# Attention plus gated FFN in one decode step: result rows by (batch, quarter of D), the FFN result moved there by fp32 selection matmuls, one store

## The chip, the cores and the metric

The kernel runs on one core of a Trainium2 chip. The metric is the device time of one execution in microseconds (us); less is better. Five runs of the kernel before gave a median of 120.75 us, from 120.64 to 121.13.

## What is computed

There are 8 batch rows of one token each, D = 512. The row is normalised, then used twice: for attention over the last 1024 positions of a K/V cache (32 query heads on 8 K/V heads of width 128), and for a gated FFN (F = 1792). The result joins the two.

```python
xn = _layernorm(x, axis=-1)                       # x: (8, 1, 512), bf16
# _A_ref: q = xn @ wq; softmax(q k^T * Dh**-0.5) v over the last W = 1024 positions; then @ wo
s = _A_ref(xn, A_k_cache, A_v_cache, A_wq, A_wo)  # wo: (4096, 512)
# _B_ref: (gelu(xn @ w_gate) * (xn @ w_up)) @ w_down     w_down: (1792, 512)
g = _silu(_B_ref(xn, B_w_gate, B_w_up, B_w_down))
return x + s * g
```

## The kernel before

**Loads.** Nearly all bytes (47.5 MB) are weights and caches that are read once. SyncE's queue (SP) issues them in one written-out order: wq and the first K slots, then V and K slots of 1 MB for 16 groups, then w_gate, w_up, w_down (1.75 MB each) and wo in six pieces of 16, 8, 4, 2, 1 and 1 rows of 128x512 (`parts`, line 488). x is loaded twice: `x_sb` for the normalisation on ScalarE's queue (line 139), and `x_res`, the x that is added at the end, on SP's queue between the second and third piece of wo (line 491).

**Order of the work.** The schedule is written by hand: every engine runs its instructions in the program's order. A prologue makes the constants and xT (the normalised x, transposed, lines 202 to 226) and q (lines 361 to 400), which is copied into `q2_all` by eight small copies (line 395). A loop over 16 groups, a group being a batch row and half of the K/V heads, turns K on TensorE (line 244), copies it (250), makes scores (270), softmax (283, 291), values (304) and normalises (lines 320 to 334). Then come `ffn_up` (403), `ffn_down` (448), and the wo product (518 to 531).

**The FFN.** `ffn_up` makes z = xn @ w_gate and u = xn @ w_up on TensorE (411), in between regroups the attention output into `og`, one 32-column block for each of the 32 row blocks of wo (353), then applies gelu on ScalarE and VectorE (423 to 435) and transposes the product into `hT`, 14 blocks of 128x32 (438). `ffn_down` multiplies the 14 blocks with w_down. The 512 columns of the result are cut in halves t: half 0 goes to PSUM partitions 0 to 31 and half 1 to partitions 64 to 95, by matmuls on different column groups of the array (`tile_position=(0, 64 * t)`, line 453), so a pair can be in the array together. Silu (465 to 474) is done once for each half on 8 partitions and gives `g_sb`.

**wo and the end.** For each row block j of wo, two matmuls of 256 columns (line 523) add to `s_ps`, half 0 on partitions 0 to 63 and half 1 on 64 to 127, with a 64-column stationary `og[:, j : j + 2, :]`. Two VectorE operations on 128 partitions multiply by the gate and add x (534, 535), and two stores write the halves, 8 rows of 512 B each, on SP's and ScalarE's queue (537, 538).

Of the kernel before, what the change touches and what calls it, by code (L numbers as in the profile page):

```python
# [8 lines left out]
ACT = mybir.ActivationFunctionType  # L9
ALU = mybir.AluOpType  # L10
AX = mybir.AxisListType
BF16 = mybir.dt.bfloat16
FP32 = mybir.dt.float32
# [3 lines left out]
def kernel(  # L17
# [13 lines left out]
    nc = tc.nc  # L31

    B, Sq, D = A_x.shape
# [11 lines left out]
    P = nc.NUM_PARTITIONS  # L45
# [10 lines left out]
    FR = F // P  # L56

    consts = ctx.enter_context(tc.tile_pool(name="consts", bufs=1))
# [21 lines left out]
        return wide.tile([P, 2 * SLOT], BF16, name="wide_slot", align_bytes=512)  # L80

    x_flat = A_x.flatten_outer_dims()
    x_sb = persist.tile([B, D], BF16, name="x_sb")
    x_res = persist.tile([P, D // 2], BF16, name="x_res")
    nc.gpsimd.memset(x_res, 0.0)

# [29 lines left out]
    def load_wo(j0, j1):  # L118
# [13 lines left out]
    k_t[1] = load_kv(A_k_cache, *groups[1])  # L132


    eps_sb = consts.tile([B, 1], FP32, name="eps_sb")
    nc.vector.memset(eps_sb, 1e-5)
    rstd = persist.tile([B, 1], FP32, name="rstd")
    nc.scalar.activation(out=rstd, in_=eps_sb, func=ACT.Sqrt)
    nc.scalar.dma_start(out=x_sb, in_=x_flat)


    ident = consts.tile([P, P], BF16, name="ident")
# [56 lines left out]
    )  # L199


    stats = persist.tile([B, nc.vector.BN_STATS_DIM], FP32, name="stats")
    nc.vector.bn_stats(out=stats, in_=x_sb)
    mv = persist.tile([B, nc.vector.BN_AGGR_DIM], FP32, name="mv")
    nc.vector.bn_aggr(out=mv, in_=stats)
    nc.scalar.activation(out=rstd, in_=mv[:, 1:2], func=ACT.Sqrt, bias=eps_sb, scale=1.0)
    nc.vector.reciprocal(out=rstd, in_=rstd)
    xhat = persist.tile([32, D], BF16, name="xhat")
    nc.vector.memset(xhat, 0.0)
    nc.vector.tensor_scalar(  # L210
        out=xhat[0:B, :],
        in0=x_sb,
        scalar1=mv[:, 0:1],
        scalar2=rstd[:, 0:1],
# [15 lines left out]
    q2_all = persist.tile([P, NHALF, B, 2, 2, HN, rep], BF16, name="q2_all")  # L230
    nc.gpsimd.memset(q2_all, 0.0)
    oT_all = persist.tile([P, B, Hq], BF16, name="oT_all")
    og = persist.tile([P, NOR + 1, 32], BF16, name="og")
    nc.vector.memset(og, 0.0)

# [105 lines left out]
    def regroup():  # L341

        zt = ffn_sb.tile([P, B * Hq], BF16, name="zt")
        nc.vector.transpose(out=zt, in_=oT_all.rearrange("p b h -> p (b h)"))
        rg = ps_a.tile([P, B, 32], FP32, name="rg_ps", tag="a")
        nc.tensor.matmul(
            rg.rearrange("p b j -> p (b j)"),
            perm,
            zt,
            start=True,  # L350
            stop=True,
        )
        nc.vector.tensor_copy(
            out=og[:, 0:NOR, 0:B], in_=rg.rearrange("p b j -> p j b")
        )


# [25 lines left out]
    for i in range(NHALF):  # L383
        qT_ps = ps_t.tile([P, rep, 2, HN, 32], BF16, name="t_ps", tag="t")
        for j in range(rep):
            for e in range(2):
                nc.tensor.transpose(
                    qT_ps[:, j, e, :, :].rearrange("p n b -> p (n b)"),
                    q_sb[:, i, j, e, :, :].rearrange("p r w -> p (r w)"),
                    ident,  # L390
                )
        for e in range(2):
            for rr in range(2):
                copy = nc.scalar.copy if rr else nc.vector.tensor_copy
                copy(  # L395
                    out=q2_all[64 * rr : 64 * rr + 64, i, :, e, rr, :, :].rearrange(
                        "p b n j -> p j n b"
                    ),
                    in_=qT_ps[64 * rr : 64 * rr + 64, :, e, :, 0:B],
                )  # L400


    def ffn_up():
        z_ps = ps_big.tile([P, 512], FP32, name="big")
        u_ps = ps_big.tile([P, 512], FP32, name="big")
        for ps, ws in ((z_ps, wg_t), (u_ps, wu_t)):
            if ps is u_ps:
                regroup()
            for k in range(NDC):
                for j in range(4):  # L410
                    nc.tensor.matmul(  # L411
                        ps[32 * j : 32 * j + 32, 0:FT],
                        xT[:, k, :],
                        ws[:, k * F + j * FT : k * F + (j + 1) * FT],
                        start=(k == 0),
                        stop=(k == NDC - 1),
                        tile_position=(0, 32 * j),
                        skip_group_check=True,
                    )
        zT = z_ps[:, 0:FT]  # L420
        uT = u_ps[:, 0:FT]
        z2 = ffn_sb.tile([P, FT], FP32, name="z2")
        nc.scalar.activation(out=z2, in_=zT, func=ACT.Square)
        nc.vector.tensor_scalar(
            out=z2, in0=z2, scalar1=0.044715, scalar2=1.0, op0=ALU.mult, op1=ALU.add
        )
        u3 = ffn_sb.tile([P, FT], FP32, name="u3")
        nc.vector.tensor_tensor(out=u3, in0=z2, in1=zT, op=ALU.mult)
        nc.scalar.activation(out=z2, in_=u3, func=ACT.Tanh, scale=0.7978845608028654)
        nc.vector.tensor_scalar(  # L430
            out=z2, in0=z2, scalar1=0.5, scalar2=0.5, op0=ALU.mult, op1=ALU.add
        )
        nc.vector.tensor_tensor(out=u3, in0=z2, in1=zT, op=ALU.mult)
        h_sb = ffn_sb.tile([P, FT], BF16, name="h_sb")
        nc.vector.tensor_tensor(out=h_sb, in0=u3, in1=uT, op=ALU.mult)

        hT = ffn_sb.tile([P, FR, 32], BF16, name="hT")
        nc.vector.transpose(
            out=hT.rearrange("p j b -> p (j b)"),
            in_=h_sb.rearrange("b (p j) -> b j p", j=FR),  # L440
        )
        return hT

    x_b = persist.tile([P, D // 2], BF16, name="x_b")
    g_sb = persist.tile([P, D // 2], FP32, name="g_sb")
    nc.vector.memset(g_sb, 0.0)

    def ffn_down(hT):
        f_ps = ps_big.tile([P, 512], FP32, name="big")
        for j in range(FR):  # L450
            for t in range(2):
                c0 = j * D + t * 256
                nc.tensor.matmul(  # L453
                    f_ps[64 * t : 64 * t + 32, 0:256],
                    hT[:, j, :],
                    wd_t[:, c0 : c0 + 256],
                    start=(j == 0),
                    stop=(j == FR - 1),
                    tile_position=(0, 64 * t),
                    skip_group_check=True,  # L460
                )
        th2 = ffn_sb.tile([P, 256], FP32, name="th2")
        for t in range(2):
            a, z = 64 * t, 64 * t + B
            nc.scalar.activation(
                out=th2[a:z, :], in_=f_ps[a:z, 0:256], func=ACT.Tanh, scale=0.5
            )
            nc.vector.tensor_scalar(
                out=th2[a:z, :], in0=th2[a:z, :], scalar1=0.5, scalar2=0.5,
                op0=ALU.mult, op1=ALU.add,  # L470
            )
            nc.vector.tensor_tensor(
                out=g_sb[a:z, :], in0=th2[a:z, :], in1=f_ps[a:z, 0:256], op=ALU.mult
            )


    for g in range(NGR + 1):
# [8 lines left out]
        if g == NGR:  # L486

            parts = [(0, 16), (16, 24), (24, 28), (28, 30), (30, 31), (31, 32)]
            wo_t = [load_wo(*q) for q in parts[:2]]
            for t in range(2):  # L490
                nc.sync.dma_start(
                    out=x_res[64 * t : 64 * t + B, :], in_=x_flat[:, t * 256 : (t + 1) * 256]
                )
            wo_t += [load_wo(*q) for q in parts[2:]]
        if g < NGR:
            score(g)
# [12 lines left out]
        if g:  # L509
            gather(g - 1)  # L510

    hT = ffn_up()
    ffn_down(hT)

    nc.vector.tensor_copy(out=x_b, in_=x_res)


    s_ps = ps_big.tile([P, 512], FP32, name="big")
    for q, (j0, j1) in enumerate(parts):
        for j in range(j0, j1):  # L520
            for t in range(2):
                c0 = (j - j0) * D + t * 256
                nc.tensor.matmul(  # L523
                    s_ps[64 * t : 64 * t + 64, 0:256],
                    og[:, j : j + 2, :].rearrange("p m b -> p (m b)"),
                    wo_t[q][:, c0 : c0 + 256],
                    start=(j == 0),
                    stop=(j == NOR - 1),
                    tile_position=(0, 64 * t),
                    skip_group_check=True,  # L530
                )
    tmp = ffn_sb.tile([P, 256], BF16, name="tmp")
    out_sb = ffn_sb.tile([P, 256], BF16, name="out_sb")
    nc.vector.tensor_tensor(out=tmp, in0=s_ps[:, 0:256], in1=g_sb, op=ALU.mult)
    nc.vector.tensor_tensor(out=out_sb, in0=tmp, in1=x_b, op=ALU.add)
    out_flat = out.flatten_outer_dims()
    nc.sync.dma_start(out=out_flat[:, 0:256], in_=out_sb[0:B, :])
    nc.scalar.dma_start(out=out_flat[:, 256:512], in_=out_sb[64 : 64 + B, :])


# [28 lines left out]
```

The softmax here doesn't subtract the row's maximum and nothing guards it: scores larger than these inputs give would overflow.

## Time and profile before

| | |
|---|---|
| median of 5 runs (lowest, highest) | 120.75 us (120.64, 121.13) |
| the profiled execution | 121.13 us, of which its span 119.5 us |
| mean granted TensorE clock | 0.90 |
| HBM read | 47.46 MB, 397 GB/s over the span |
| busy: TensorE, VectorE, ScalarE | 87.8, 64.2, 40.5 us |
| share of DMA in the chain that ended last | 52% |

In the profile's lines, times are us from the start of the span. PE is TensorE's matmuls, PEld its weight loads, DVE is VectorE, ACT ScalarE, POOL GpSimd, SPq and ACTq the queues that issue DMAs. "L523" is line 523 of the kernel, "x28" a count of instructions, and the bracket at the end of a line tells how long the engine had been idle and what it waited for. A row of 40 digits cuts the span in 40 slices of 3 us: the digit is a busy share in tenths, and for PEclk the clock that TensorE was granted in tenths of the full one. In a table by stretches, each engine's busy time is followed by its count of instructions; the last three columns are the granted clock, the DMA share and GB/s.

### The profile page before, as it was taken

Reading aid. Unit: us, or ns where it says so; the run is one execution under the profiler, and the core shown is the slowest. Engines: PE = TensorE matmul, PEld = TensorE weight load, DVE = VectorE, ACT = ScalarE, POOL = GpSimd, SP = SyncE. Lnnn points to the kernel's source line nnn. Section 1 sums busy time; section 2 is a strip of 40 time slices with the busy share of each in tenths; the row PEclk is TensorE's granted clock in tenths of the full one; section 3 lists DMA queues with packets and bytes.
Section 4 is the critical chain, followed back from the end, with each engine's and each line's share of the span. In section 5 each row is a group of like instructions: output and inputs, shape, how many; then the busy total and the mean of one; then the engine's idle time right before and its main releaser. Section 6 shows DMA issues by size and latency. Waiting matters only on the chain.

```text
span 119.5 us, 2281 instructions
## 1 busy us (share of the span) xinstructions
PE 87.8 (74%) x929; PEld 63.1 (53%) x929; DVE 64.2 (54%) x149; ACT 40.5 (34%) x78; POOL 4.3 (4%) x10
## 2 busy tenths in 40 slices
PE   0014966676999999999998797977979840554990
PEld 0004723453867876786776584665847620142870
DVE  5250644735567866866695574845847426512201
ACT  4000314692433562464355342362433303002000
POOL 7600000000000000000000000000000000000000
PEclk9999999769599999999999999999999985555579
DMA  4999999999999999999999999999999999999920
GB/s 93 431 400 461 400 431 425 428 428 422 425 428 431 422 417 431 425 428 420 428 425 428 422 422 431 431 414 428 431 431 441 418 432 446 425 430 406 397 105 3
DMA packets 6281, 47.61 MB, mean 398 GB/s; under 512 B 728, under 2 KB 1024, under 8 KB 1280
## 3 DMA queue, kind: packets, MB, share of 16 engines
q1 hardware_dynamic: 6240, 47.46, 94.7%
q8 instruction: 7, 0.11, 0.3%
q10 hardware_dynamic: 32, 0.01, 0.0%
q14 instruction: 2, 0.02, 0.0%
HBM read 47.46 MB, written 0.01 MB: 397 GB/s over the span
## 4 chain that ended last, share of the span: by engine, by line
DMA 52%; PE 29%; DVE 10%; ACT 4%; issue 1%; SPq 0%; DVEq 0%
DMA wide_slot<-in_B_w_gate_dram 18%; DMA slot<-in_A_v_cache_dram 16%; PE t_ps L244 13%; DMA wide_slot<-in_A_wo_dram 10%; DMA slot<-in_A_k_cache_dram 8%; DVE kT L250 6%; PE big L523 5%; PE sc_ps L270 4%; PE o_ps L304 3%; ACT q_all L395 2%; PE big L366 2%; DVE q_all L395 2%; ACT L283 1%; PE big L411 1%; DVE q_sb L379 1%
## 5 line engine op out<-in xcount | busy, mean ns | idle before, releaser
L250 DVE COPY kT<-t_ps 128x1024 bf16<-128x1024 bf16 x48 | 31.8, 687 | 25.2 <-PE t_ps L244 23.3
L244 PE MATMUL t_ps<-ident_f,slot 128*128 128x128 f32 x256 | 38.6, 300 | 7.0 <-DMA slot<-in_A_k_cache_dram 6.8
L244 PEld LDWEIGHTS t_ps<-ident_f,slot 128*128 128x128 f32 x256 | 30.7, 152 | 17.2 <-issue 6.8
L250 ACT COPY kT<-t_ps 128x1024 bf16<-128x1024 bf16 x16 | 16.2, 1012 | 15.1 <-PE t_ps L244 14.7
L283 ACT ACTIVATE p<-sc_ps 128x512 bf16<-128x512 f32 x16 | 9.6, 597 | 29.2 <-PE sc_ps L270 29.1
L270 PE MATMUL sc_ps<-kT,q_all 128*32 128x512 bf16 x128 | 10.1, 384 | 4.2 <-ACT q_all L395 1.8
L291 DVE STREAM_TRANSPOSE pT<-p 128x512 bf16<-128x512 bf16 x16 | 11.3, 703 | 3.1 <-ACT p L283 3.1
L304 PE MATMUL o_ps<-slot,pT 128*32 128x256 bf16 x256 | 10.4, 284 | 0.0
L324 PE MATMUL a_ps<-selr,o_sb 128*128 128x16 f32 x64 | 9.7, 264 | 0.4 <-ACT o_sb L314 0.3
L324 PEld LDWEIGHTS a_ps<-selr,o_sb 128*128 128x128 f32 x64 | 8.5, 194 | 0.6 <-ACT o_sb L314 0.6
L270 PEld LDWEIGHTS <-q_all 128*32 128x32 bf16 x128 | 3.2, 94 | 8.1 <-issue 3.2
L304 PEld LDWEIGHTS <-pT 128*32 128x32 bf16 x256 | 5.6, 97 | 2.8 <-issue 2.4
L314 ACT COPY o_sb<-o_ps 128x256 f32<-128x256 f32 x16 | 6.0, 377 | 1.3 <-PE o_ps L304 1.3
L523 PEld LDWEIGHTS <-og 128*64 128x64 bf16 x64 | 4.8, 151 | 2.8 <-DMA wide_slot<-in_A_wo_dram 2.1
L260 PE MATMUL sc_ps<-far,hot 4*128 4x512 bf16 x16 | 6.2, 385 | 0.0
L411 PE MATMUL big<-wide_slot,xT 128*32 128x448 bf16 x32 | 2.9, 503 | 4.2 <-DMA wide_slot<-in_B_w_up_dram 2.7
L220 PE MATMUL t_ps<-ident,xhat 32*128 32x32 bf16 x4 | 0.3, 194 | 7.2 <-DVE xhat L210 7.2
L320 PEld LDWEIGHTS a_ps<-ss,ones_f 128*128 128x128 f32 x32 | 5.1, 200 | 0.5 <-DVE oT_all L334 0.3
L453 PE MATMUL big<-wide_slot,hT 128*32 128x256 bf16 x28 | 3.2, 416 | 2.6 <-DMA wide_slot<-in_B_w_down_dram 2.6
L320 PE MATMUL a_ps<-ss,ones_f 128*128 128x16 f32 x32 | 5.1, 234 | 0.0
L523 PE MATMUL big<-wide_slot,og 128*64 128x256 bf16 x32 | 3.6, 420 | 1.6 <-DMA wide_slot<-in_A_wo_dram 1.6
L333 DVE RECIPROCAL rs<-a_ps 128x16 f32<-128x16 f32 x16 | 4.0, 250 | 1.4 <-PE a_ps L324 1.2
(64 smaller groups left out, 51.1 us busy)
## 6 DMA issues: line engine op xcount, KB each, us to landing
slot<-in_A_k_cache_dram SPq DMA_DIRECT2D x16, 1024.0 KB, 19.6
slot<-in_A_v_cache_dram SPq DMA_DIRECT2D x16, 1024.0 KB, 19.6
wide_slot<-in_A_wq_dram SPq DMA_DIRECT2D x2, 2048.0 KB, 13.5
wide_slot<-in_A_wo_dram SPq DMA_DIRECT2D x1, 2048.0 KB
wide_slot<-in_B_w_gate_dram SPq DMA_DIRECT2D x1, 1792.0 KB, 21.4
wide_slot<-in_B_w_up_dram SPq DMA_DIRECT2D x1, 1792.0 KB, 23.2
wide_slot<-in_B_w_down_dram SPq DMA_DIRECT2D x1, 1792.0 KB, 25.0
slot<-in_A_wo_dram SPq DMA_DIRECT2D x1, 1024.0 KB
```

The costliest lines, as they stand in the source:

```text
L244: nc.tensor.transpose(kp[:, c * P : (c + 1) * P], kw[:, rp * P : (rp + 1) * P], ident_f)
L250: copy(out=kT_t[g][:, t * 8 * P : (t + 1) * 8 * P], in_=kp.bitcast(BF16))
L260: nc.tensor.matmul(sc, hot.rearrange("n r q -> n (r q)"), far, start=True, stop=False, skip_group_check=True,)
L270: nc.tensor.matmul(sc[32 * t : 32 * t + 32, :], q2_all[:, i, b, e, :, :, :].rearrange("w r n j -> w (r n j)"), kT[:, :, 32 * t : 32 * t + ...
L283: nc.scalar.activation(out=p, in_=sc_t[g], func=ACT.Exp, scale=inv_sqrt_dh, accum_out=acc)
L291: nc.vector.transpose(out=pT, in_=p)
L304: nc.tensor.matmul(o_ps[32 * u : 32 * u + 32, :], pT_t[g][:, m * 32 : (m + 1) * 32], v_t[g][:, m * 256 : (m + 1) * 256], start=(m < 4), st ...
L314: nc.scalar.copy(out=o_sb, in_=o_ps)
L320: nc.tensor.matmul(a_ps[:, 0, :], ones_f, ss_t[g], start=True, stop=True, skip_group_check=True)
L324: nc.tensor.matmul(a_ps[:, 1, :], o_t[g][:, r * Dh : (r + 1) * Dh], selr[:, r, :], start=(r == 0), stop=(r == 1), skip_group_check=True,)
L395: copy(out=q2_all[64 * rr : 64 * rr + 64, i, :, e, rr, :, :].rearrange("p b n j -> p j n b"), in_=qT_ps[64 * rr : 64 * rr + 64, :, e, :, 0:B],
L523: nc.tensor.matmul(s_ps[64 * t : 64 * t + 64, 0:256], og[:, j : j + 2, :].rearrange("p m b -> p (m b)"), wo_t[q][:, c0 : c0 + 256], start= ...
```

## The change

The result is held on 32 partitions, one for each (batch, quarter of D), row 4b + q, in place of 8 batch rows with two halves of D on two groups of partitions.

- **x.** `x_sb` has 32 rows, of which every fourth holds a batch row; VectorE fills it with zeros first, and it is loaded by two issues on ScalarE's queue. So `xhat`, and the copies that took columns 0 to 7 of a 32-column block, work with every fourth column (lines 353 and 395). `x_res` holds x in the (batch, quarter) form, loaded by two issues of 16 rows of 256 B. Its memset and the copy `x_b` go.
- **Shifted stationaries.** `og` keeps batch b in column 4b of a block. A 32-column window that begins q columns earlier puts batch b into output row 4b + q. So each row block of wo is multiplied by four matmuls of 128 columns, one for each quarter, all adding to the same 32x128 result.
- **Even rows in an own tile.** Row blocks 0, 2, ... 26 add to a second PSUM tile on partitions 32 to 63 (column group 32), all others, with 28 to 31, to a first one on partitions 0 to 31. An even and the next odd row block take turns. The even half is multiplied by the gate and gets x added (`early`) ahead of the last sum.
- **FFN result.** `ffn_down` makes 14 matmuls of 512 columns on one column group. The 32x512 result is copied to SBUF in fp32 by ScalarE, and four fp32 matmuls with a shifted identity (`push`, made by GpSimd) move its quarters to rows 4b + q. Silu is then done once, on 32x128.
- **One store** of 32 rows of 256 B.

```diff
-    x_sb = persist.tile([B, D], BF16, name="x_sb")
-    x_res = persist.tile([P, D // 2], BF16, name="x_res")
-    nc.gpsimd.memset(x_res, 0.0)
+    NQ = 32 // B
+    DQ = D // NQ
+    x_sb = persist.tile([32, D], BF16, name="x_sb")
+    nc.vector.memset(x_sb, 0.0)
+    x_res = persist.tile([32, DQ], BF16, name="x_res")
+    x_rows = x_flat.rearrange("b (q c) -> (b q) c", q=NQ)
...
-    nc.scalar.dma_start(out=x_sb, in_=x_flat)
+    for t in range(2):
+        c = slice(t * D // 2, (t + 1) * D // 2)
+        nc.scalar.dma_start(out=x_sb[0:32:NQ, c], in_=x_flat[:, c])
...
-    nc.vector.memset(xhat, 0.0)
     nc.vector.tensor_scalar(
-        out=xhat[0:B, :],
+        out=xhat,
...
+    push = consts.tile([32, 32 + NQ - 1], FP32, name="push")
+    nc.gpsimd.memset(push, 0.0)
+    nc.gpsimd.tensor_copy(out=push[:, NQ - 1 :], in_=ident[0:32, 0:32])
...
-            out=og[:, 0:NOR, 0:B], in_=rg.rearrange("p b j -> p j b")
+            out=og[:, 1:, 0:32:NQ], in_=rg.rearrange("p b j -> p j b")
...
-                    in_=qT_ps[64 * rr : 64 * rr + 64, :, e, :, 0:B],
+                    in_=qT_ps[64 * rr : 64 * rr + 64, :, e, :, 0:32:NQ],
...
+    def shifted(t, j, q):
+        return t.rearrange("p j b -> p (j b)")[:, 32 * (j + 1) - q : 32 * (j + 2) - q]
+
+    def ffn_down():
         f_ps = ps_big.tile([P, 512], FP32, name="big")
         for j in range(FR):
-            for t in range(2):
...
+            nc.tensor.matmul(
+                f_ps[0:32, :],
+                hT[:, j, :],
+                wd_t[:, j * D : (j + 1) * D],
+                start=(j == 0),
+                stop=(j == FR - 1),
+                tile_position=(0, 0),
+                skip_group_check=True,
             )
+        f_sb = ffn_sb.tile([32, D], FP32, name="f_sb")
+        nc.scalar.copy(out=f_sb, in_=f_ps[0:32, :])
+        f_ps = ps_a.tile([P, DQ], FP32, name="f2_ps", tag="a")
+        for q in range(NQ):
+            nc.tensor.matmul(
+                f_ps[0:32, :],
+                push[:, NQ - 1 - q : NQ - 1 - q + 32],
+                f_sb[:, q * DQ : (q + 1) * DQ],
+                start=(q == 0),
+                stop=(q == NQ - 1),
+                skip_group_check=True,
             )
+        th2 = ffn_sb.tile([32, DQ], FP32, name="th2")
+        nc.scalar.activation(out=th2, in_=f_ps[0:32, :], func=ACT.Tanh, scale=0.5)
+        nc.vector.tensor_scalar(
+            out=th2, in0=th2, scalar1=0.5, scalar2=0.5, op0=ALU.mult, op1=ALU.add
+        )
+        nc.vector.tensor_tensor(out=g_sb, in0=th2, in1=f_ps[0:32, :], op=ALU.mult)
...
+                r = slice(16 * t, 16 * t + 16)
+                nc.sync.dma_start(out=x_res[r, :], in_=x_rows[r, :])
...
+    s_ps = [ps_big.tile([P, 512], FP32, name="big") for _ in range(2)]
+    acc = [s_ps[0][0:32, 0:DQ], s_ps[1][32:64, 0:DQ]]
+    side = [int(j % 2 == 0 and j < NOR - 4) for j in range(NOR)]
+    where = {j: (q, j0) for q, (j0, j1) in enumerate(parts) for j in range(j0, j1)}
+    for pair in [(j, j + 1) for j in range(0, NOR - 2, 2)] + [(NOR - 2,), (NOR - 1,)]:
+        for q in range(NQ):
+            for j in pair:
+                a = side[j]
+                rows = [m for m in range(NOR) if side[m] == a]
+                piece, j0 = where[j]
+                c0 = (j - j0) * D + q * DQ
                 nc.tensor.matmul(
-                    s_ps[64 * t : 64 * t + 64, 0:256],
-                    og[:, j : j + 2, :].rearrange("p m b -> p (m b)"),
-                    wo_t[q][:, c0 : c0 + 256],
+                    acc[a],
+                    shifted(og, j, q),
+                    wo_t[piece][:, c0 : c0 + DQ],
...
-                    tile_position=(0, 64 * t),
+                    tile_position=(0, 32 * a),
...
-    nc.vector.tensor_tensor(out=tmp, in0=s_ps[:, 0:256], in1=g_sb, op=ALU.mult)
-    nc.vector.tensor_tensor(out=out_sb, in0=tmp, in1=x_b, op=ALU.add)
-    out_flat = out.flatten_outer_dims()
-    nc.sync.dma_start(out=out_flat[:, 0:256], in_=out_sb[0:B, :])
-    nc.scalar.dma_start(out=out_flat[:, 256:512], in_=out_sb[64 : 64 + B, :])
+    nc.vector.tensor_tensor(out=early, in0=acc[1], in1=g_sb, op=ALU.mult)
+    nc.vector.tensor_tensor(out=early, in0=early, in1=x_res, op=ALU.add)
+    nc.vector.tensor_tensor(out=tmp, in0=acc[0], in1=g_sb, op=ALU.mult)
+    nc.vector.tensor_tensor(out=out_sb, in0=tmp, in1=early, op=ALU.add)
+    nc.sync.dma_start(
+        out=out.flatten_outer_dims().rearrange("b (q c) -> (b q) c", q=NQ), in_=out_sb
+    )
```

## The prediction

> **What bounds the kernel now.** I read first the page's 40 slices, then the chain that ended last, then the timeline of the last 15 us, then busy time and granted clock by stretches.
>
> ```profile
> PEclk9999999769599999999999999999999985555579
> DMA  4999999999999999999999999999999999999920
> ```
>
> ```profile
> 98.51 12.02 DMA wide_slot<-in_A_wo_dram
> 110.53 0.04 issue
> 110.57 5.76 PE big L523 x57
> 116.34 0.02 issue
> 116.36 0.44 DVE tmp L534
> 116.80 0.02 issue
> 116.82 0.29 DVE out_sb L535
> ```
>
> The DMA engines are full to slice 38, so up to some 114 us the transfers set the time, and only the tail can be won or lost. In the chain the wo transfer is followed by 5.76 us of matmuls of line 523: TensorE starts wo when its first piece lands (110.53) and is behind when the last does. That last piece is issued at 105.69 and takes 9.9 us (DMA issues), so it is there at about 115.6, and TensorE ends at 116.32. The row PEclk says why it is behind: half clock from slice 35 on.
>
> ```profile
> 105.81 3.17 PE L453 MATMUL big<-wide_slot,hT 128*32 128x256 bf16 x28 [2.62 <-DMA wide_slot<-in_B_w_down_dram]
> 109.02 0.37 ACT L465 ACTIVATE th<-big 8x256 f32<-8x256 f32 x1 [8.19 <-PE big L453]
> ...
> 110.57 3.62 PE L523 MATMUL big<-wide_slot,og 128*64 128x256 bf16 x32 [1.59 <-DMA wide_slot<-in_A_wo_dram]
> ...
> 117.14 0.32 SPq L537 DMA_DIRECT2D out_dram<-out_sb  x1
> ```
>
> ```profile
> 104.59:108.00 3.41, 2.19 (x22) 1.81 (x24) 0.28 (x1) 0.00 (x0) 0.00 (x0) 0.50 1.02 439
> 108.00:111.41 3.41, 1.82 (x18) 1.14 (x16) 1.39 (x4) 0.75 (x2) 0.00 (x0) 0.50 0.96 398
> 111.41:114.83 3.42, 3.42 (x36) 2.84 (x32) 0.23 (x1) 0.00 (x0) 0.00 (x0) 0.50 0.83 322
> 114.83:118.24 3.41, 1.49 (x28) 1.20 (x22) 0.72 (x2) 0.00 (x0) 0.00 (x0) 1.00 0.05 14
> ```
>
> In these stretches the second number is TensorE's busy time, the one ahead of the DMA share the clock. Means of short stretches give the times at which it changed (0.67 from 114.5 to 115.0: a third of it at full clock, so 114.83): 22.67, 26.08, 29.49, 32.91, 97.76 and 114.83, all on a grid of 3.41 us. It rose after stretches that were busy for 3.21 of 3.41 us or more, and did not after 2.19 of 3.41.
>
> **Rates.** Two 256-column matmuls on different column groups go together: 14 of line 523 from 110.57 take 1.70 us, less 0.42 for the last one, over 6 steps: 213 ns a pair at half clock. At full clock the 16 of line 304 (four groups) take 0.62, less 0.28, over 3 steps: 112 ns. A column thus costs 0.83 ns at half and 0.44 ns at full clock. For 128 columns the five transposes of line 387 (from 18.12, 0.45 us, less 0.23, over 4) give 56 ns; half clock would be 107.
>
> **The change, part by part.**
>
> *Front end.* x is loaded in two issues on ACT's queue (0.58 us the one now) behind a VectorE memset of x_sb (about the 0.27 us of line 209, which goes). xT is 0.5 to 0.9 us later. It was ready at 7.8; TensorE's next work starts at 10.62, when K lands, and xT's reader at 14.22. Hidden by 2.8 us; without that cover, 0.9. Behind the two issues ScalarE has only the square root that needs x anyway. POOL loses a 0.31 us memset and gains a small memset and a copy after 4.96, when it has nothing left; their reader runs at 112. The eight q_all copies (0.73 us each) read every fourth column: between no change (the elements are the same, so no gain) and double (+5.8 us in all). I take nothing: line 353, which reads with a stride, needs 425 ns for 256 elements, the contiguous line 472 412. The chain from there runs on TensorE to 56 us and then on DMA, whose loads are issued some 19.6 us before they land; this cover holds even the doubling. The og copy now writes strided (0.43 us, at worst double); hT was ready at 104.9, w_down at 105.8, so 0.9 us covers it. x_res stays at its place on SP's queue, two issues of 16 short rows for two of 8; without its memset nothing is awaited; no reader before 116.
>
> *FFN down.* 28 matmuls of 256 columns, two at a time, become 14 of 512 on one column group. At half clock 14 x 427 ns = 5.98 us in place of 3.17. By the profile's grid the stretch 108.00 to 111.41 is now wholly busy, so the clock rises at 111.41, inside the fourteenth: the result is there at 111.8 (0.2 us for the last result to come out), not 108.98.
>
> *Moving it.* ScalarE copies 32x512 from PSUM. Lines 314 (256 elements, 377 ns) and 423 (448, 544) give 0.87 ns an element: 0.60, with two handovers of 0.04 to 0.05. Then four fp32 matmuls of 128 columns. Line 320 has 32 records for 16 calls, so an fp32 matmul counts twice; line 244 moves 128 fp32 columns in 110 ns (five from 36.17 in 0.71 us, less 0.27, over 4 steps). 8 x 0.11 = 0.88 us. Bounds: 8 x 0.056 = 0.45 and, at half clock, 1.75. Behind them on TensorE waits all of wo, which now starts at 113.4, not 110.57; tanh and gate follow (0.26 + 0.21 + 0.30) and end near 114.5, needed at 116.7.
>
> *wo.* 128 matmuls of 128 columns for 64 of 256. Rows 0 to 27 go in pairs on two groups: 14 x 4 steps; rows 28 to 31 all on one group: 16 steps. 72 x 56 ns = 4.03 us, at full clock now; before, it was 32 pairs, 18 or so of them at half clock. Last result 0.16 later: 117.6 against 116.32. The steps are bounded below by the columns (56 ns) and above by the weight load that goes ahead of each matmul: line 304's take 97 ns, so 72 x 97 = 7.0 us, +3.0. I take 56, because line 387 gets it with loads of 98 ns beside each matmul and line 304 issues four pairs of load and matmul in 112 ns. The Trainium skill (TensorE: Matmul & The Clock Gate, "Back-to-back issue gap") speaks against that: a stream of load and matmul pairs holds some 81 ns at 128 columns. As an estimate from that page, 72 x 81 ns would be 5.8 us, ending 1.8 us later than my sum.
>
> *Last arithmetic and store.* Before: 0.43 + 0.29 and handovers from 116.32 to 117.14 = 0.82. After: the even half is multiplied and x added (0.30 + 0.19 + 0.1, from 116.7 to 117.3) under the 16 steps of rows 28 to 31; uncovered they would cost 0.25 at most. Left is one product of 128 columns from PSUM (lines 534 and 428 give 1.02 ns an element: 0.30) and one sum (between 0.175, line 334, and 0.293, line 535; I take 0.19), with handovers 0.59: a gain of 0.23. One store of 32 rows of 256 B for two of 8 rows of 512 B on two queues: its 2.34 us from issue to the end lie between -0.2 (the second queue's wait goes) and +0.3 (its issue once more); I take 0. The same skill (DMA: Bandwidth & Descriptors, "Specifications") holds pieces under 512 B slow; no transfer of this trace shows it, and my sum has nothing for it.
>
> **Sum.** 117.6 + 0.59 = 118.2 for the store's issue, against 117.14: +1.05 us. On the profiled execution (121.13; span 119.5 and 1.6 around it) 122.2. The median is 0.38 lower. The three lower runs fit a clock that rose early enough for wo to end with its last piece (0.46 us less). The same earlier grid, by 0.6 us, would shorten the new down by 0.3. So 121.8 to 121.9 for a median run: I say **121.8**.
>
> **Rivals.**
> 1. *The clock rises early in the 6 us block (the other side).* If 2.3 to 2.9 busy us are enough and the grid lies well, it rises near 108.4, down ends at 110.3, wo starts at 111.9 at full clock and catches up with its transfer: 115.6 + 4 x 0.056 + 0.16 = 116.0. Then 0.3 + 0.23 us are won: 120.5 on the profiled execution, 120.2 on the median. It decides where wo starts before 112.0. For it: a solid block where now there are gaps. Against: 2.19 of 3.41 was not enough, and grid points at 108.0 and 111.41 lie badly. 8%. A rise between (108.8 to 110) gives 120.5 to 121.1: 17%.
> 2. *The clock stays low past the down.* If the copy's pause, or work on 32 columns, keeps it down to the next point, selection costs 1.75 and wo runs partly at 107 ns a step: wo starts at 114.4, four steps to 114.83, 68 x 56 ns, end 118.8: 123.3 profiled, 123.0 median; a full stretch more gives 125. For it: no stretch of the trace shows one group alone. Against: 22.67 to 26.08 had a gap and was enough. 10%.
> 3. *Weight loads show.* 81 to 97 ns a step: 123.6 to 125. 6%.
> 4. *It doesn't do what it says:* the even rows end early but their arithmetic is not hidden. +0.1 to +0.25, inside the forecast.
>
> **How the numbers follow.** Forecast (121.3 to 122.5) 59%, rivals 8, 17, 10 and 6%. The measurement tells 0.3% (0.36 us) from no change: below 120.39 8%, 120.39 to 121.11 17%, above 75%. The range drops most of rival 1 and the upper part of 2 and 3: 120.4 to 123.4.
>
> **What would show it.** Line for the down: 14 matmuls over 5 to 6 us with wo's first one near 113, and no wait of TensorE for wo's first piece; four selection matmuls in 0.9 us; wo in some 4.2 us at clock 1.00, ending 1 us or more after the last piece lands; 0.59 us from there to the store. Wrong if wo ends at the last landing, if the clock rises before 109, or if a step takes over 65 ns.

## The result and the profile after

The kernel after takes 121.51 us (median of 28 runs, 120.96 to 123.40), the kernel before 120.77 us (median of 49, 120.54 to 121.31). The ratio is 1.0065, with a 95% interval of 1.0050 to 1.0079: slower by 0.7 us. Two runs of after (123.06 and 123.40, over 1.5% above its fastest) count as slow and are left out of the ratio; the longest of the others took 122.43. The profiled execution of after took 121.88 us, of which the span is 120.1 (before: 121.13 and 119.5).

Not all of the loss lies in the span. What a run takes outside it is 1.75 us in after and 1.67 in before (means of time less span: 1.66 to 1.68 in every version with before's wo, 1.74 to 1.88 in every one with after's). So about 0.1 of the 0.7 us is outside the span; no term of the prediction has it, and what makes it was not tried.

Two rows of the page of after, the granted clock and the DMA share in 40 slices:

```profile
PEclk9999999677699999999999999999999965555999
DMA  4999999999999999999999999999999999999910
```

The transfers end where they did, in slice 38. The clock is different: it is low for five slices, not six, and is full again from slice 38 on. Two stretches of after show where it rises:

```profile
107.19:110.60 3.41, 3.41 (x10) 1.21 (x9) 0.00 (x0) 0.00 (x0) 0.00 (x0) 0.50 0.97 413
...
109.00:112.00 3.00, 2.35 (x7) 0.70 (x5) 0.00 (x0) 0.57 (x1) 0.00 (x0) 0.73 0.98 410
```

The mean of 0.73 over 3 us is 1.6 us at half clock and 1.4 at full clock, so it rose at 110.60, behind 3.41 us in which the FFN product kept TensorE busy without a pause. So the last work of TensorE, which ran half at low clock before, now runs at full clock, and still ends later. The chain that ended last in after, from 90 us on (start, length, what):

```profile
80.63 25.07 DMA wide_slot<-in_B_w_down_dram
...
105.83 5.54 PE big L462 x14
...
111.39 0.58 ACT f_sb L472
...
112.11 1.03 PE f_ps L475 x8
113.14 4.14 PE big L541 x128
...
117.30 0.29 DVE tmp L555
...
117.62 0.28 DVE out_sb L556
```

Left out are five lines "issue" of 0.02 to 0.14 us. The last transfer in the chain is now that of w_down, not of wo. Behind it stand four things of TensorE and ScalarE with no wait for a transfer between them: the product (line 462), the copy (472), the move (475) and all of wo (541). Three lines of the timeline of after show that wo waits for nothing (no bracket) and when the store is issued:

```profile
113.07 1.96 PE L541 MATMUL big<-wide_slot,og 128*32 128x128 bf16 x64
114.87 2.40 PE L541 MATMUL big<-slot,og 128*32 128x128 bf16 x64
...
117.92 0.35 SPq L557 DMA_DIRECT2D out_dram<-out_sb  x1
```

wo's first matmul is at 113.07 (before 110.57). The last piece of wo has landed at 115.57, and TensorE ends 1.7 us behind it (before: 0.8, 116.34 against 115.55). Before and after, term by term in the two profiled executions: end of wo 116.34 to 117.28, +0.94; from there to the issue of the store 0.80 to 0.64, -0.16; from the issue to the end of the span 2.34 to 2.18, -0.16. The sum is +0.62, the difference of the spans; the two times differ by 0.75, the rest being outside the span.

### The profile page after: what moved, and what is told of

Read it like the earlier page. It is cut to its first block, busy times and chain, and to the rows that moved or that the text cites. A ratio compares the mean times of both kernels' runs of the same rounds, so it can differ in the third digit from the quotient of the medians.

```text
span 120.1 us, 2395 instructions
## 1 busy us (share of the span) xinstructions
PE 89.7 (75%) x987; PEld 63.2 (53%) x987; DVE 63.4 (53%) x147; ACT 40.6 (34%) x78; POOL 4.2 (4%) x11
## 4 chain that ended last, share of the span: by engine, by line
DMA 45%; PE 35%; DVE 11%; ACT 5%; issue 2%; SPq 0%; DVEq 0%
DMA wide_slot<-in_B_w_down_dram 21%; DMA slot<-in_A_v_cache_dram 16%; PE t_ps L255 15%; DMA slot<-in_A_k_cache_dram 8%; DVE kT L261 7%; PE big L462 5%; PE sc_ps L281 4%; PE o_ps L315 4%; PE big L541 3%; ACT q_all L406 2%; DVE q_all L406 2%; PE big L377 2%; ACT L294 1%; PE f_ps L475 1%; DVE q_sb L390 1%
## 5 line engine op out<-in xcount | busy, mean ns | idle before, releaser
L255 PEld LDWEIGHTS t_ps<-ident_f,slot 128*128 128x128 f32 x256 | 31.4, 155 | 14.2 <-issue 8.3
L462 PE MATMUL big<-wide_slot,hT 128*32 128x512 bf16 x14 | 5.5, 581 | 2.7 <-DMA wide_slot<-in_B_w_down_dram 2.7
L422 PE MATMUL big<-wide_slot,xT 128*32 128x448 bf16 x32 | 3.4, 573 | 3.8 <-DMA wide_slot<-in_B_w_up_dram 2.2
L462 PEld LDWEIGHTS <-hT 128*32 128x32 bf16 x14 | 1.9, 140 | 6.6 <-DVE hT L448 3.4
```

Of the source, the lines that this page charges most:

```text
L255: nc.tensor.transpose(kp[:, c * P : (c + 1) * P], kw[:, rp * P : (rp + 1) * P], ident_f)
L462: nc.tensor.matmul(f_ps[0:32, :], hT[:, j, :], wd_t[:, j * D : (j + 1) * D], start=(j == 0), stop=(j == FR - 1), tile_position=(0, 0), ski ...
```

## The experiments

Ratios are to the kernel before in the same job. Its medians there: 120.80 (experiments 1 to 4), 120.76 (5 to 8) and 120.75 us (9 to 12).

The theory: wo begins 2.5 us late behind product, copy and move, and its 72 steps of 56 ns (a pair of matmuls on two groups, or one of rows 28 to 31) don't fit between that start and the last landing. Rivals: the product on one group alone costs it; the front end costs it; the number of steps doesn't matter, because weight loads or the clock set the pace.

**1. The FFN product on four column groups, the move in one matmul** (`e1_down4`).

```diff
+            for q in range(NQ):
                 nc.tensor.matmul(
-                f_ps[0:32, :], hT[:, j, :], wd_t[:, j * D : (j + 1) * D],
+                    f_ps[32 * q : 32 * q + 32, 0:DQ], hT[:, j, :],
+                    wd_t[:, j * D + q * DQ : j * D + (q + 1) * DQ],
...
-        f_sb = ffn_sb.tile([32, D], FP32, name="f_sb")
+        f_sb = ffn_sb.tile([P, DQ], FP32, name="f_sb")
```

`push` becomes a 128x32 selection, used once.

> The changed kernel, but the four quarters of the FFN product go to four column groups (14 x 4 matmuls of 128 columns) and one fp32 matmul with a 128-row selection moves them. Theory (the loss is the serial stretch ahead of wo: 5.5 us of one-group product, 0.6 copy, 1.0 moving): the stretch shrinks to 14 x 107 ns + 0.3 copy + 0.5 moving, some 2.7 us at half clock, done by 108.6; wo starts when its first piece lands, 110.5, but now at half clock for part of its 72 steps (107 ns each), so the end is 116.0 to 117.5 in place of 117.3: a median of 121.0, between 120.4 and 121.6. Rival A (wo's own 72 steps or the store set the loss, the stretch is nothing): unchanged at 121.5. Rival B (the clock is all: the long product pays for itself by raising the clock): no better or worse than 121.5, with wo's steps at 107 ns.

Measured: 121.31 us (7 runs, 120.62 to 122.00), ratio 1.0050 [1.0021, 1.0079]. Its timeline:

```profile
105.91 1.68 PE L465 MATMUL big<-wide_slot,hT 128*32 128x128 bf16 x56 [2.62 <-DMA wide_slot<-in_B_w_down_dram]
...
108.05 0.60 PE L477 MATMUL f_ps<-f_sb,push 128*32 128x128 f32 x2 [0.46 <-ACT f_sb L475]
...
110.69 3.60 PE L538 MATMUL big<-wide_slot,og 128*32 128x128 bf16 x64 [2.04 <-DMA wide_slot<-in_A_wo_dram]
```

Product and move are over 4.5 us earlier, and wo starts when its first piece lands. But the first 64 matmuls, 32 steps, take 3.60 us: 107 ns a step, half clock. The clock rose at 114.53 only, and wo ended at 116.71. In this execution the earlier start gave back most of what it won, because the shorter product no longer brings the clock back.

**2. The product in two halves on two groups** (`e2_down2`), two copies, the same move.

```diff
+            for t in range(2):
                 nc.tensor.matmul(
-                f_ps[0:32, :],
+                    f_ps[64 * t : 64 * t + 32, 0:256],
...
-        nc.scalar.copy(out=f_sb, in_=f_ps[0:32, :])
+        nc.scalar.copy(out=f_sb[:, 0:256], in_=f_ps[0:32, 0:256])
+        nc.vector.tensor_copy(out=f_sb[:, 256:512], in_=f_ps[64:96, 0:256])
```

> The changed kernel, but the FFN product is made as before, in two halves of 256 columns on two groups (two copies side by side on ScalarE and VectorE follow, moving unchanged). Theory: product 3.2 us, ends at 109.0, copies to 109.5, the four fp32 matmuls 0.9 (full clock) to 1.75 us (half), wo from 110.5 to 111.4, end between 116.0 and 117.2: median 121.0, between 120.5 and 121.5. Rival A (the one-group product costs nothing): 121.5.

Measured: 121.56 us (11 runs, 120.83 to 121.85), ratio 1.0057 [1.0041, 1.0074]: a miss, no gain. In the chain of its profiled execution:

```profile
114.40 0.55 PE big L544 x13
114.95 0.42 issue
115.37 1.19 PE big L544 x19
```

TensorE was ready and the data were there (the piece with rows 24 to 27 landed at 114.36). Yet between 114.73, the last start ahead of the gap, and 115.37 no matmul starts, and no semaphore explains it: the chain calls it "issue". That is something that my theory didn't have; it comes back in 5 and 12. The rest of the theory held: wo started at 110.61. Only this execution was profiled, so it is not shown that the other ten lose their time in the same way.

**3. All wo rows on one column group** (`e3_one_group`): 128 steps, no early half.

```diff
-    side = [int(j % 2 == 0 and j < NOR - 4) for j in range(NOR)]
+    side = [0 for j in range(NOR)]
...
-    nc.vector.tensor_tensor(out=out_sb, in0=tmp, in1=early, op=ALU.add)
+    nc.vector.tensor_tensor(out=out_sb, in0=tmp, in1=x_res, op=ALU.add)
```

> The changed kernel with all 32 row blocks of wo on one column group: 128 steps in place of 72, and no early part (x is added in the last sum). Theory (wo is bound by TensorE's column steps, 56 ns each at full clock): 56 more steps, +3.1 us, 124.6, with a step of 56 ns in the trace. Rival A (wo is bound by its transfers): 121.5. Rival C (steps are bound by weight loads, so that two groups share them): less than +1.

Measured: 124.93 us (6 runs, 124.34 to 125.27), ratio 1.0333 [1.0308, 1.0358]. In the chain:

```profile
112.49 7.26 PE big L541 x128
```

128 steps in 7.26 us, 56 ns each with the last result coming out. The number of steps sets wo's length. As the product is the same as in after, this execution also shows how the place of the clock's rise differs between executions. Its stretches (TensorE busy, weight loads, VectorE, ScalarE, GpSimd, clock, DMA share, GB/s):

```profile
108.00:109.00 1.00, 1.00 (x4) 0.33 (x3) 0.00 (x0) 0.00 (x0) 0.00 (x0) 0.50 0.94 401
109.00:110.00 1.00, 1.00 (x5) 0.44 (x4) 0.00 (x0) 0.00 (x0) 0.00 (x0) 0.84 0.96 410
```

The clock rises about 109.3 (0.84 is 0.32 us at half and 0.68 at full clock), and the product ends at 110.72, not 111.37.

**4. The front end alone on the kernel before** (`e4_front`): x in 32 rows, and result rows at every fourth partition, so that x_res and both stores go to and from every fourth partition.

```diff
-    nc.scalar.dma_start(out=x_sb, in_=x_flat)
+    for t in range(2):
+        c = slice(t * D // 2, (t + 1) * D // 2)
+        nc.scalar.dma_start(out=x_sb[0:32:NQ, c], in_=x_flat[:, c])
...
-    nc.sync.dma_start(out=out_flat[:, 0:256], in_=out_sb[0:B, :])
+    nc.sync.dma_start(out=out_flat[:, 0:256], in_=out_sb[0:32:NQ, :])
```

> The kernel before with the front end of the change alone: x in every fourth of 32 rows, loaded in two issues behind a memset, strided copies of q and of the attention output. Theory (hidden behind the first K and the queue of loads): 120.8, within 0.2 of before. Rival D (the later x and the strided copies delay the loads): +0.4 or more, 121.2.

Measured: 121.51 us (6 runs, 121.33 to 121.94), ratio 1.0062 [1.0043, 1.0080]: a miss, and by itself it would have made the front end the culprit. But the timeline shows what my edit added:

```profile
117.29 0.67 SPq L540 DMA_DIRECT2D out_dram<-out_sb  x1
117.29 0.70 ACTq L541 DMA_DIRECT2D out_dram<-out_sb  x1
```

The issues of the two stores take 0.67 and 0.70 us, where the contiguous ones of before take 0.32 and 0.30, and the data land 2.09 us after the issue begins in place of 1.45. That is 0.64 us at the end of the chain, which the change hasn't. Experiment 8 does it again without it.

**5. After, with filler matmuls that hold the clock** (`e5_warm_after`): 27 matmuls of 512 columns into an unread PSUM tile, in three places where TensorE waits; they compute nothing that is used.

```diff
+    def busy(n):
+        w_ps = ps_t.tile([P, 512], FP32, name="t_ps", tag="t")
+        for _ in range(n):
+            nc.tensor.matmul(w_ps, ident, ..., start=True, stop=True, skip_group_check=True)
...
+        busy(5)      # ahead of w_gate's product
+                busy(10)   # behind the regrouping
+        busy(12)     # ahead of w_down's product
```

> The changed kernel with 27 added matmuls of 512 columns into an unread tile, put in TensorE's waits for the FFN weights (5 ahead of the gate product, 10 between gate and up, 12 after up), so that its clock stays up. Theory (the product, copy and moving stretch ahead of wo, at half clock, is what starts wo late): at full clock the product takes 14 x 216 ns = 3.0 us, wo starts at 110.6 to 111 and catches up with its last piece (115.6), ending at 116.0: median 120.3, little spread. Rival E (something else holds the median up: instruction supply for the 256 matmuls and loads, or the front end): still 121.0 or more.

Measured: median 120.58 us (12 runs, 120.49 to 121.93), ratio 1.0006 [0.9977, 1.0035]. The twelve are of two kinds: eight at 120.49 to 120.70 and four at 121.59 to 121.93. The profiled one is of the long kind (121.59), and its chain says where it is lost:

```profile
99.99 14.30 DMA slot<-in_A_wo_dram
114.29 1.15 issue
115.44 1.53 PE big L557 x32
```

At full clock throughout, the product took 3.18 us, the copy and move were over by 110.75, and wo kept up with its transfers to row 23. Then TensorE stood still for 1.15 us with the next piece there, as in 2. The instruction queue has a transfer of 16 KB shortly before, from 113.03 to 113.91; it had ended 0.38 us when the standstill began. In 2 such a transfer ran from 113.14 to 114.07, 0.66 us ahead of the gap; in the profiled execution of after one ran from 113.83 to 114.71, in the midst of wo, and TensorE went on. So the traces do not show that the standstill is a wait for this transfer. With the clock held, eight runs of twelve lose nothing against before.

**6. The same fillers in the kernel before** (`e6_warm_before`).

> The kernel before with the same added matmuls. Theory: wo ends with its last piece, 115.9 in place of 115.9 to 116.3: median 120.65, spread under 0.4 us; 0.3 us above the changed kernel with the same matmuls, since its last arithmetic and two stores are longer. Rival E: unchanged at 120.8.

Measured: 120.72 us (12 runs, 120.61 to 121.82), ratio 0.9988 [0.9968, 1.0009]. wo ended at 116.03, 0.36 us behind its last piece (115.67). Before has almost nothing to win from the clock; after has (121.51 to 120.58).

**7. Experiment 1 with wo's rows on four column groups** (`e7_groups4`): rows 0 to 27 in turn on four groups, 28 to 31 on one, 44 steps in place of 72. The rows of three groups are summed early.

```diff
-    side = [int(j % 2 == 0 and j < NOR - 4) for j in range(NOR)]
+    side = [j % 4 if j < NOR - 4 else 0 for j in range(NOR)]
...
+    nc.scalar.copy(out=early, in_=acc[1])
+    nc.vector.tensor_tensor(out=early, in0=acc[2], in1=early, op=ALU.add)
+    nc.vector.tensor_tensor(out=early, in0=acc[3], in1=early, op=ALU.add)
```

> The four-group FFN product and single moving matmul of the first experiment, and wo's row blocks 0 to 27 in turn on four column groups (28 steps) with 28 to 31 on one (16 steps): 44 steps for 72, the three early tiles added while the last row blocks run. Theory (the end is TensorE's steps against the last landing): even at half clock 44 x 107 = 4.7 us from 110.6, so wo ends with its last piece, 115.6 + 0.4 + 0.2 = 116.2 whatever the clock does: median 120.5, little spread. Rival E (instruction supply): no better than the 121.3 of the first experiment, since the count of matmuls and loads is the same.

Measured: 121.40 us (9 runs, 121.26 to 121.74), ratio 1.0047 [1.0031, 1.0063]: a miss by 0.9. Two of its stretches of 3 us, columns as above:

```profile
109.00:112.00 3.00, 1.33 (x52) 1.34 (x56) 0.49 (x2) 0.00 (x0) 0.00 (x0) 0.50 0.97 397
...
115.00:118.00 3.00, 1.85 (x17) 1.58 (x15) 1.69 (x6) 0.26 (x1) 0.00 (x0) 0.50 0.01 4
```

With fewer steps TensorE is busy 1.33 of 3 us, and 2.22 in the next three, and the clock stays at 0.50 to the end. Rows 28 to 31, 16 steps that nothing hides, run at 107 ns each, and wo ends at 116.86. TensorE's waits in wo are all for transfers, so a standstill as in 2 is not the cause here. In this execution fewer steps left the last ones twice as long.

**8. The front end alone, again** (`e8_front_again`): as 4, but result rows, x_res and stores as in before; the FFN product reads every fourth column of `hT`.

```diff
+                    f_ps[64 * t : 64 * t + B, 0:256],
+                    hT[:, j, 0:32:NQ],
```

> The front end of the change alone again, on the kernel before, this time with its result rows, attention layout and stores as they were (the FFN's transposed product is read at every fourth column). In the run of the front end before this, the stores read every fourth partition, took 0.67 us to issue where they took 0.32, and landed 0.7 us later; that is left out here. Theory (the front end is hidden; the 0.7 us of that run were its stores): 120.8, within 0.2. Rival D (the later x delays the loads or the end): 121.2 or more.

Measured: 120.75 us (12 runs, 120.61 to 121.37), ratio 1.0002 [0.9986, 1.0019]. The front end is free. The two kernels differ in the placing of the result rows (og, x_res, the stores), so the 0.7 us of experiment 4 is put down to its stores, which are longer by 0.64.

**9. After without copy and move** (`e9_direct`): the product itself uses shifted stationaries, four matmuls of 128 columns for each of the 14 blocks, all on one group, straight into rows 4b + q.

```diff
-            nc.tensor.matmul(
-                f_ps[0:32, :], hT[:, j, :], wd_t[:, j * D : (j + 1) * D],
+            for q in range(NQ):
+                c0 = j * D + q * DQ
+                nc.tensor.matmul(
+                    f_ps[0:32, 0:DQ], shifted(hT, j, q), wd_t[:, c0 : c0 + DQ],
...
-        f_sb = ffn_sb.tile([32, D], FP32, name="f_sb")
-        nc.scalar.copy(out=f_sb, in_=f_ps[0:32, :])
-        f_ps = ps_a.tile([P, DQ], FP32, name="f2_ps", tag="a")
```

> The changed kernel without the move: the FFN product itself uses shifted stationaries, as wo does (14 x 4 matmuls of 128 columns on one group), so its result stands in the (batch, quarter) rows at once; no copy, no fp32 matmuls. The product is as long as in the changed kernel. Theory (what the tail loses is the copy and the move, 1.7 us, during which wo waits; the long product itself is paid back by the clock that it raises): wo starts at 110.8 to 111.7 at full clock, 72 x 56 ns end before the last piece, so it ends at 116.0: median 120.5. Rival A2 (the product on one group is the loss): little better than 121.5. Rival E (instruction supply, with 80 more matmuls and loads than the changed kernel): a part of the executions near 121.6.

Measured: 120.73 us (12 runs, 120.56 to 121.50), ratio 1.0002 [0.9979, 1.0024]: 0.78 less than after by the medians, all of its loss. Nine runs lie at 120.56 to 120.78, three at 121.31 to 121.50. The profiled one is of the three; in its chain the copy and the move are gone, but the gate stands in their place:

```profile
105.77 5.72 PE big L462 x53
...
111.70 0.28 ACT th L472
...
112.25 0.29 DVE g_sb L476
...
112.57 4.19 PE big L529 x127
```

The even rows' PSUM tile takes the place of the product's, so wo waits until the gate has read it (112.53). The clock rose at 111.26 here. The nine shorter executions were not profiled; that an earlier rise makes them is only argued.

**10. The kernel before with its product on one group** (`e10_before_one_group`): 14 matmuls of 512 columns.

```diff
-            for t in range(2):
...
-                    f_ps[64 * t : 64 * t + 32, 0:256],
...
+                f_ps[0:32, :],
+                hT[:, j, :],
+                wd_t[:, j * D : (j + 1) * D],
```

> The kernel before with one part of the change: the FFN product as 14 matmuls of 512 columns on one group (the gate's second half is read from the other columns). Theory (the product's 2.4 us more are paid back by the clock): the product ends at 110.8 to 111.8, wo's 32 pairs then run at 109 ns and end with the last piece, 115.9: median 120.75, within 0.2 of before. Rival A2 (the product on one group is the loss): wo ends 0.7 or more later, 121.4.

Measured: 120.83 us (12 runs, 120.59 to 121.16), ratio 0.9995 [0.9975, 1.0016]. Its chain:

```profile
106.01 6.03 PE big L451 x14
112.04 3.70 PE big L521 x62
```

The product is 2.9 us longer and wo begins 1.5 us later, and nothing is lost: the clock rose at 111.8, wo's pairs ran at full clock and were ready for the last piece when it landed (115.73), ending at 116.09. The longer product pays for itself.

**11. Experiment 7 with the fillers** (`e11_groups4_warm`).

> The four-group kernel with the added matmuls that hold the clock up. Without them its clock stayed at 0.50 from 98 us to the end and the sixteen steps of row blocks 28 to 31 took 107 ns each, 1.7 us. Theory (clock): at 56 ns they take 0.9 us, wo ends at 115.6 + 0.4 = 116.0: median 120.45, 0.9 below the same kernel without them. Rival E (instruction supply): a part of the executions near 121.6 again, as with the changed kernel and these matmuls (8 near 120.55, 4 near 121.7).

Measured: 121.40 us (12 runs, 120.85 to 121.61), ratio 1.0038 [1.0017, 1.0059]: a miss by 0.95. Its stretches:

```profile
106.00:109.00 3.00, 1.32 (x58) 0.91 (x58) 0.49 (x2) 0.53 (x2) 0.00 (x0) 1.00 0.99 423
109.00:112.00 3.00, 1.25 (x60) 1.25 (x64) 0.00 (x0) 0.00 (x0) 0.00 (x0) 0.85 0.98 402
```

The fillers held the clock to 111.1; then the quick product and the wait for wo (1.32 and 1.25 of 3 us busy) lost it again, and rows 28 to 31 again took 107 ns a step; here too TensorE's waits in wo are for transfers. By the grid of this execution, TensorE was busy for 0.44 of the 3.41 us ahead of the fall. My fillers stood ahead of the FFN's products, not where this kernel waits.

**12. Experiment 5 with TensorE's instructions moved along** (`e12_warm_pad`): 24 small matmuls into an unread tile in the prologue, so that all later ones stand 48 places later in TensorE's stream.

```diff
+    for _ in range(24):
+        nc.tensor.matmul(pad_ps[:, 0:64], ident, ident[:, 0:64], start=True, stop=True, ...)
     for t in range(4):
         turn_k(0, t)
```

> The changed kernel with the added matmuls, and 24 small matmuls more in the prologue, where TensorE waits anyway, so that every later TensorE instruction stands 48 places further on in its stream. In the run without them TensorE stood still for 1.15 us with its data there, after an instruction fetch at 113.03. Rival E (the standstill is instruction supply, tied to a place in the stream): it moves to another place or goes, and the share of executions near 121.7 changes from a third to none or to nearly all. If it is chance or the DMA rings: about a third near 121.7 again.

Measured: 120.68 us (12 runs, 120.55 to 120.75), ratio 0.9986 [0.9967, 1.0004]; none of the twelve is near 121.7. In its chain the last 32 matmuls begin as their piece lands:

```profile
114.28 1.67 PE big L562 x32
```

wo ends at 115.95, 0.44 us behind its last piece. The long runs of 5 are gone with the places of the instructions (four of twelve, then none), as the rival of instruction supply foresaw. It is weak support. Were the versions alike, all four long runs would fall among the twelve of 5 about once in 21 times. The added matmuls also changed other things: in the profiled execution the clock was low from 94.01 to 100.84 (in 5 it was full from 31.5 us on), and wo began at 111.28, not 110.68. And in 2 and 5 the instruction transfer had ended before the standstill. Its cause stays open.

No version beats the kernel before by a margin outside its interval; the best, 12, is at 0.9986 [0.9967, 1.0004].

## Why the prediction was right

The forecast was 121.8 us, slower by some 1 us; measured is 121.51, slower by 0.7. The mechanism is the one forecast: wo starts late behind product, copy and move, and ends by TensorE's own pace behind the last landing. Step by step, in the profiled execution:

- **FFN product.** Forecast: 14 x 427 ns with the rise at 111.41, done at 111.8. The records are 427 ns apart as forecast, but the clock rose at 110.60 and the end was 111.37. I took the grid of 3.41 us from before's execution; it lies elsewhere in each (about 109.3 in experiment 3, 111.8 in 10); it is partly luck that this term came within 0.5 us. The spans of after's executions lie between 119.2 and 120.7 us, which fits this; that it makes the spread was not shown one by one. The longer product by itself costs nothing (10), which the prediction, adding up terms, didn't say: it brings the clock back 4 us earlier than before (110.60 against 114.83), and wo gets that back.
- **Copy and move.** Copy 0.575 us against 0.60. Move: 8 records, 109 ns apart, as forecast, 1.03 against 0.88 us, since the sum had left out the time in which the last result comes out (0.16). wo began at 113.07 against 113.4. These two steps are what the change could have done without: without them the layout is level with before (9).
- **wo.** 72 steps at 56 ns, 4.03 us, and 0.17 for the last result, as forecast; end 117.28 against 117.6, by the earlier start alone. The weight loads (97 ns records) are hidden under the matmuls. The rule of the Trainium skill (TensorE: Matmul & The Clock Gate, "Back-to-back issue gap"), 81 ns a matmul at 128 columns, did not hold here: 56 ns on one column group (3), and two matmuls in 56 ns on two.
- **Last arithmetic.** The early half (116.41 to 117.00) lay under the last 16 steps, as forecast. The final sum took 0.28 us, not 0.19, and so the stretch 0.64 and not 0.59. Of the two rows that bounded it (0.175 and 0.293) I had taken a value by the lower one; the upper, the sum that it replaces, was near.
- **Store.** Forecast 0; measured -0.16 from issue to the end, of which 0.07 is an earlier landing (1.38 us after the issue began, 1.45 before). The Trainium skill (DMA: Bandwidth & Descriptors, "Specifications") puts the least size for line rate at 512 B. This store, in pieces of 256 B, shows no cost of it.
- **Front end.** The cost was 0 as forecast (8), but the delay was mis-sized: xT was ready at 10.77, 3.0 us later, where 0.5 to 0.9 was forecast. The timeline of after's first 15 us:

```profile
1.26 1.38 ACTq L145 DMA_DIRECT2D x_sb<-in_A_x_dram  x1
...
8.24 0.68 DVE L209 BATCH_NORM_STATS2 stats<-x_sb 32x6 f32<-32x512 bf16 x1 [5.17 <-DMA x_sb<-in_A_x_dram]
...
10.54 0.23 DVE L231 COPY xT<-t_ps 128x128 bf16<-128x128 bf16 x1 [0.41 <-PE t_ps L225]
10.61 3.68 PE L255 MATMUL t_ps<-ident_f,slot 128*128 128x128 f32 x16
```

The two issues take 1.38 and (from 2.67 on) 0.64 us where one took 0.58, and the second half of x, issued behind more of the weights than the one load was, lands late: the statistics start at 8.24, not 4.97. The cover I named, 2.8 us, is used up to the last tenth: the transposes of xhat end just ahead of the first K turn (10.61; before 10.62). The copies into `q_all` are unchanged (0.72 to 0.73 us), so reading every fourth column costs nothing; the copy into `og`, which writes so, took 0.73 for 0.43, hidden.

- **From the profiled execution to the median.** I took 0.38 us off because before's profiled execution lies that far above its median. After's lies 0.37 above its own, but nothing in the runs says that it had to. The time outside the span, taken as unchanged, grew by 0.1. One reading was off by a slice: in before's row PEclk half clock begins with slice 34, not 35; no term rests on it.

**The rivals.** *The clock rises early:* not in the profiled execution, whose clock rose after 109 and whose wo began at 113.07, where this rival decides from 112.0. That it lies differently in others speaks for part of this rival: 6 of the 28 runs of after are at 121.11 or less, the outer part that I gave 17%, and none is at 120.39 or less. Its condition, that 2.3 to 2.9 busy us are enough, is met in part: 2.76 were enough in 8 and 2.88 in 2, while 3.08 (7) and 3.19 (12) were not. *The clock stays low past the product:* not in this execution; a product that keeps TensorE less busy does it (1, 7). *Weight loads show:* no, 56 ns a step. *It doesn't do what it says:* the even rows' arithmetic was hidden.

**Where the change's gain went.** The tail is shorter by 0.32 us (0.16 + 0.16). Against it stands the end of wo, later by 0.94. With the clock held up and no standstill wo ends 0.44 us behind its last piece (12), near the 0.36 of before with fillers (6); what is left is 120.68 against 120.72 us, no difference that these runs can tell. Their spans do differ, 118.85 against 119.0 us by the medians; the 0.1 us outside the span takes most of that back.

## What to carry to other kernels

Work put between a transfer's landing and the next stage delays that stage only as far as it isn't waiting for its own transfer anyway; what counts is when the stage ends against its last landing, here 1.7 us behind it in place of 0.8. TensorE's clock rose here behind busy stretches, so a shorter stage can leave the one behind it at half clock: add up a stage's time together with the clock that it leaves to the next (experiments 1, 7, 10 and 11). And before an experiment is believed, look for what its own edit added at the end of the chain (experiment 4's stores).

## What the runs showed of the hardware

- **The granted clock changes on a grid of 3.41 us, which lies differently in each execution.** In every profiled execution its changes are whole multiples of 3.41 us apart. It rose after stretches in which TensorE was busy throughout (3.41 of 3.41 us in after, 1, 3, 9 and 10) and not after 2.19 (before). In between, TensorE's busy time in one stretch does not settle it: it rose after 2.76 (8) and 2.88 (2), and not after 3.08 (7, at 26.44) and 3.19 (12, at 97.42). For the fall it settles less: it fell after 0.44 (11), 1.46 (12, at the end) and 1.77 (before), but also after 3.08 (12, at 94.01), and stayed up after 1.52 (6) and 2.09 (5). What decides there is not known. With wo cut to 44 steps it stayed at 0.50 to the end (7).
- **TensorE stood still with data present**: 0.64 us (2) and 1.15 us (5). In both a 16 KB instruction transfer had ended 0.66 and 0.38 us earlier; in after one ran during wo and TensorE went on. With its instructions moved along by 48 places, none of 12 runs had the longer time (12). The cause stays open.
- **DMAs to or from every fourth partition took longer to issue**: 0.67 and 0.70 us for 0.32 and 0.30 (8 rows of 512 B, experiment 4), landing 0.64 us later. The two such loads of x in after took 1.38 and 0.64 us, where the one load of 8 rows of 1 KB took 0.58; why the first is the longer was not tried.
- **An fp32 matmul of 128 columns is two records, 109 ns apart, at full clock** (move of after).
